# Prologue of a fused attention and MLP kernel: GpSimd normalises the third chunk by add and multiply, two constants are made sooner, and the sums of two tiles stand ahead of their squares

## The chip, the core and the metric

The kernel runs on one core of a Trainium2 chip. A core has five engines that run at the same time, each with its own instruction queue: PE (TensorE, matrix products), DVE (VectorE), ACT (ScalarE), POOL (GpSimd) and SP (SyncE, which here only issues DMAs). An engine takes its instructions strictly in the order in which they stand in its queue; an instruction that waits for another engine holds up everything behind it. The metric is the device time of one execution in microseconds (us), lower is better. Before the change it is 777.7 us, the median of three runs that went from 776.79 to 778.06 us.

## What is computed

The input `x` has 2048 tokens of 512 numbers. The reference is, cut to what matters:

```python
xn = layernorm(x)                                  # over the 512 numbers of a token
q, k, v = heads(xn @ wqkv)                         # 32 heads of 16 numbers
scores = q @ k.T / 4, only for 0 <= i - j < 256    # causal, sliding window of 256 tokens
s = softmax(scores) @ v  (heads joined)  @ wo
g = silu(gelu(layernorm(xn) @ w1 + b1) @ w2 + b2)  # 512 -> 1792 -> 512
out = x + s * g
```

Here only the first line, the projections of the first heads and the first row maxima of their scores matter.

## The kernel before

**Stages.** The tokens are worked on in 4 chunks of 512, a chunk in 4 tiles of 128 tokens (the partitions). The stages are a prologue (some 77 us: layernorm of all chunks, their transposes, the first projections), the attention of eight groups of four heads (to about 420 us), then the MLP and the output. The order on every engine but SP is fixed by hand: instructions stand on their engine in the order in which the program issues them. The prologue runs in time steps `t` = -16 to -1, four for each chunk; `fills` holds the PE work of each step, `plan`, `lns` and `ends` other work at given steps. In step `t` the row maxima of block `m = t + 12` are also made (`max_block`, line 469).

**Numbers in two parts.** Products are made of a high and a low part of each operand. So an array that PE has put into PSUM is copied by ACT (the high part) and then DVE subtracts that from the original (the low part). For a chunk of `xn` these are the ACT `CAST xnT` and the DVE `TENSOR_TENSOR xnT` of the profile.

**Layernorm** (`layernorm`, line 81) gives a tile's steps in one of three ways:

- By DVE's statistics (`each`, line 107): DVE finds mean and variance (`mv`), POOL takes the power -1/2 (`rs`); then `end` (line 139) has ACT, DVE or POOL apply them. For tiles in `on_pool` POOL does it: `(x - mean) * rs`, subtract and multiply, in the profile `x<-x,mvA,rsA`. These are tiles 1 to 3 of the third chunk.
- By sums (`by_sums`): `total` (line 89) has ACT sum the tile and POOL make the negative mean `nm` of it; `squares` (line 94) has ACT sum the squares of `x + nm` and POOL make `rs` of that (`ve`, then a power); `end_sums` (line 101) has POOL make `(x + nm) * rs`, add and multiply, in the profile `x<-x,nmA,rsA`. Tiles 0 and 1 of the second chunk, tile 0 of the third and all four of the last are made so.

The steps of the last chunk (`ln3`) run at `lns` (line 772): tiles 0 and 1 at the end of step -13, tiles 2 and 3 at the end of step -11, each tile's three steps in a row.

**The prologue's buffers.** Chunks 3 and 4 lie in one SBUF tile, `x23`. The transposes of a chunk (`job_x`, line 232) go into PSUM tiles `tr` of a pool of two buffers (`ps_st`, line 190), into `fb`, and for one chunk `zo`; the first halves of V (`job_v`, line 335, PE `pv`, then an ACT copy into `vt`) take turns on the same two `ps_st` buffers. So a `pv` waits until the two parts of the transposes before it are taken out of PSUM, and a transpose waits until the `pv` before it is copied.

**Row maxima** (`max_block`). PE puts scores of a block of 128 queries into `xy` (older keys into `zo`), DVE replaces those above the diagonal (`copy_predicated`, line 488, with the triangle `upper` as the mask) and takes the maximum (`mt<-xy`). Each block overwrites `xy`, so PE waits for the maximum of the block before.

**The two constants.** `upper` begins as all ones: PE multiplies it with itself in 16 products at the start, whose result nobody reads, and ACT copies it into the first q/k slot. Line 690 then makes the triangle of it on POOL. Line 689 puts ones into the last column of `vt`, whose first reader is `clear_part` (line 211) at step -4.

Of the kernel before, what the change touches and what calls it, by code (L numbers as in the profile page):

```python
# [13 lines left out]
ALU = mybir.AluOpType  # L14
# [3 lines left out]
S, D, H, DH, WIN, F = 2048, 512, 32, 16, 256, 1792  # L18
P = 128
# [30 lines left out]
def mixer_kernel(ctx, tc, x, wqk, wv, wo, w1, b1, w2, b2, out):  # L50


    nc = SimpleNamespace(**{name: Ordered(tc, name) for name in ("tensor", "vector", "scalar", "gpsimd", "sync")})
# [27 lines left out]
    def layernorm(ts, name, on_act, eager=False, n_act=4, by_sums=(), on_pool=()):  # L81

        n = len(ts)
        nm = small.tile([P, n], F32, tag="nm", name=f"nm{name}") if by_sums else None
        sums = small.tile([P, n, 2], F32, tag="sums", name=f"sums{name}") if by_sums else None

        def total(i):

            nc.scalar.activation(x23[:, 8], ts[i], AF.Identity, accum_out=sums[:, i, 0:1])
            nc.gpsimd.tensor_scalar(nm[:, i: i + 1], sums[:, i, 0:1], -1.0 / D, None, op0=ALU.mult)

        def squares(i):

            nc.scalar.activation(x23[:, 8], ts[i], AF.Square, bias=nm[:, i: i + 1], accum_out=sums[:, i, 1:2])
            ve = small.tile([P, 1], F32, tag="ve1", name=f"ve{name}_{i}")
            nc.gpsimd.tensor_scalar(ve, sums[:, i, 1:2], 1.0 / D, EPS, op0=ALU.mult, op1=ALU.add)
            nc.gpsimd.tensor_tensor(rs[:, i: i + 1], ve, mhalf[:, :1], op=ALU.pow)

        def end_sums(i):
            nc.gpsimd.tensor_scalar(ts[i], ts[i], nm[:, i: i + 1], rs[:, i: i + 1], op0=ALU.add, op1=ALU.mult)
        mv = small.tile([P, n, 2], F32, tag="mv", name=f"mv{name}")
        rs = small.tile([P, n], F32, tag="rs", name=f"rs{name}")
        sh = small.tile([P, n], F32, tag="shift", name=f"shift{name}")

        def each(i):

            stats(i)
            ve = small.tile([P, 1], F32, tag="ve1", name=f"ve{name}_{i}")  # L110
            nc.vector.tensor_scalar(ve, mv[:, i, 1:2], EPS, None, op0=ALU.add)
            nc.gpsimd.tensor_tensor(rs[:, i: i + 1], ve, mhalf[:, :1], op=ALU.pow)

        def shift(i):
            nc.vector.scalar_tensor_tensor(sh[:, i: i + 1], mv[:, i, 0:1], -1.0, rs[:, i: i + 1],
                                           op0=ALU.mult, op1=ALU.mult)

        def stats(i):
            st = small.tile([P, 6], F32, tag="bn", name=f"bn{name}_{i}")
            nc.vector.bn_stats(st, ts[i])  # L120
            nc.vector.bn_aggr(mv[:, i], st)

        def invert():
            ve = small.tile([P, n], F32, tag="ve", name=f"ve{name}")
            nc.vector.tensor_scalar(ve, mv[:, :, 1], EPS, None, op0=ALU.add)
            nc.gpsimd.tensor_tensor(rs, ve, mhalf[:, :n], op=ALU.pow)

        def shift_all():
            if on_act:
                nc.vector.scalar_tensor_tensor(sh, mv[:, :, 0], -1.0, rs, op0=ALU.mult, op1=ALU.mult)  # L130

        def apply(i, on_act=on_act):
            if on_act:
                nc.scalar.activation(ts[i], ts[i], AF.Identity, bias=sh[:, i: i + 1], scale=rs[:, i: i + 1])
            else:
                nc.vector.tensor_scalar(ts[i], ts[i], mv[:, i, 0:1], rs[:, i: i + 1],
                                        op0=ALU.subtract, op1=ALU.mult)

        def end(i):

            if i in on_pool:
                nc.gpsimd.tensor_scalar(ts[i], ts[i], mv[:, i, 0:1], rs[:, i: i + 1], op0=ALU.subtract, op1=ALU.mult)
                return
            if i < n_act:
                shift(i)
            apply(i, i < n_act)
        if eager:
            return [(lambda i=i: total(i), lambda i=i: squares(i), lambda i=i: end_sums(i)) if i in by_sums else
                    (lambda i=i: each(i), lambda i=i: end(i)) for i in range(n)]
        return [lambda i=i: stats(i) for i in range(n)] + [invert, shift_all] + [lambda i=i: apply(i) for i in range(n)]  # L150
# [48 lines left out]
    vt = vp.tile([P, NKB, 16, DH + 1], F32, name="vt")  # L199
# [16 lines left out]
    upper = const.tile([P, P], F32, name="upper")  # L216
# [39 lines left out]
    def halves(dst_hi, dst_lo, src, part):  # L256

        if part != 1:
            nc.scalar.copy(dst_hi, src)
        if part != 0:  # L260
            nc.vector.tensor_sub(dst_lo, src, dst_hi.bitcast(F32))

    def split_wqk(part=None):
        n, raw = raws["qk"]
        if part != 1:
            wqs[n] = bigp.tile([P, 2, KT, P], F32R, tag=f"wb{n % 2}", name=f"wqb{n}")
        halves(wqs[n][:, 0], wqs[n][:, 1], raw, part)
# [379 lines left out]
    def transpose0(i):  # L647
        for kt in range(KT):
            nc.tensor.transpose(tr0[kt][:, P * i: P * (i + 1)], xs[0][i][:, P * kt: P * (kt + 1)], ident)
        for _ in range(3 if i < 3 else 0):  # L650
            nc.tensor.matmul(zo[:, 0, 0:P], ident, ident, start=True, stop=True)
# [6 lines left out]
            transpose0(i - 1)  # L658
    ln[3][1]()
    transpose0(3)  # L660
    split_wqk(0)
    ln1 = layernorm(xs[1], "A1", True, True, 3, by_sums=(0, 1))
    ln2 = layernorm(xs[2], "A2", True, True, by_sums=(0,), on_pool=(1, 2, 3))
    ln3 = layernorm(xs[3], "A3", True, True, by_sums=range(4))
# [21 lines left out]
        ln2[i][0]()  # L686
    for i in range(4):
        ln2[i][-1]()
    nc.gpsimd.memset(vt[:, :, :, DH: DH + 1], 1.0)
    nc.gpsimd.affine_select(out=upper, in_=upper, pattern=[[1, P]], compare_op=ALU.is_gt,  # L690
                            fill=0.0, base=0, channel_multiplier=-1)
    for i in range(8):
        behind(-14 + i // 4, nc.sync.dma_start, xn_d[i], xs[i // 4][i % 4])

# [74 lines left out]
    fills[16 * NQ, 0] = [(first_h, (0,))]  # L769
    at(16 * NQ, activate_first)  # L770

    lns = {-13: [*ln3[0], *ln3[1]], -11: [*ln3[2], *ln3[3]]}

    def fill_in(t, half):
        now[:] = t, half
# [56 lines left out]
    for f in range(6, NF, 2):  # L832
        t = gp.tile([P, 2, 512], F32, tag="ohl", name=f"hr_{f}", bufs=4)
# [421 lines left out]
```

## Time and profile before

| | before |
|---|---|
| median of three runs | 777.7 us (776.79 to 778.06) |
| span of the profiled execution, first to last instruction | 775.7 us |
| PE busy | 750.1 us, 97% |
| DVE, ACT, POOL busy | 526.2, 437.5, 295.2 us |
| mean granted PE clock | 0.991 |

The profile shows one execution; its span is 2.0 us below the median of the runs, which also hold what lies around the first and the last instruction. A row of the timeline gives start, length, engine, operation, result and operands with shapes, and in brackets how long the engine was idle before and whom it waited for; consecutive rows of one engine may overlap by some hundredths. All rows have the line number of a helper (L42), so they are told apart by their tiles. The table by windows gives each engine's busy time within a stretch, then PE's granted clock as a share of full speed and the DMA engines' busy share.

### The profile page before, as it was taken

Reading aid. Unit: us, or ns where it says so; the run is one execution under the profiler, and the core shown is the slowest. Engines: PE = TensorE matmul, PEld = TensorE weight load, DVE = VectorE, ACT = ScalarE, POOL = GpSimd, SP = SyncE. Lnnn points to the kernel's source line nnn. Section 1 sums busy time; section 2 is a strip of 40 time slices with the busy share of each in tenths; the row PEclk is TensorE's granted clock in tenths of the full one; section 3 lists DMA queues with packets and bytes.
Section 4 is the critical chain, followed back from the end, with each engine's and each line's share of the span. In section 5 each row is a group of like instructions: output and inputs, shape, how many; then the busy total and the mean of one; then the engine's idle time right before and its main releaser. Section 6 shows DMA issues by size and latency. Waiting matters only on the chain.

```text
span 775.7 us, 18801 instructions
## 1 busy us (share of the span) xinstructions
PE 750.1 (97%) x7428; PEld 586.2 (76%) x7428; DVE 526.2 (68%) x834; ACT 437.5 (56%) x742; POOL 295.2 (38%) x591
## 2 busy tenths in 40 slices
PE   9789999999999999999999999999999999999997
PEld 8678666676668887666666677888887888888886
DVE  6567677786876777988876446754647676576473
ACT  6535776777766676678776865444546454342001
POOL 7710666657656465665875810030100200000101
PEclk9879999999999999999999999999999999999999
DMA  7622444765446883455644274541202322243531
GB/s 258 188 54 49 102 97 114 163 149 117 110 92 167 263 259 99 109 130 140 168 142 155 70 250 147 183 167 41 82 9 82 128 68 96 82 150 123 175 95 54
DMA packets 56951, 99.40 MB, mean 128 GB/s; under 512 B 11104, under 2 KB 11360, under 8 KB 56864
## 3 DMA queue, kind: packets, MB, share of 16 engines
q1 hardware_dynamic: 56864, 98.21, 44.0%
q8 instruction: 58, 0.95, 0.5%
q14 instruction: 29, 0.24, 0.1%
HBM read 51.39 MB, written 29.62 MB: 104 GB/s over the span
## 4 chain that ended last, share of the span: by engine, by line
PE 85%; ACT 4%; POOL 4%; DVE 4%; issue 2%; DMA 1%; DVEq 0%; ACTq 0%; POOLq 0%
PE acc L42 19%; PE fb L42 18%; PE zo L42 12%; PE p L42 9%; PE stb L42 8%; PE h L42 6%; PE s L42 6%; PE xy L42 5%; ACT pt L42 3%; PE pv L42 2%; POOL x L42 1%; POOL pt L42 1%; DVE xy L42 1%; POOL rsA L42 1%; DVE mt L42 1%
## 5 line engine op out<-in xcount | busy, mean ns | idle before, releaser
L42 POOL TENSOR_SCALAR_AFFINE_SELECT pt<-pt 128x256 f32<-128x256 f32 x480 | 193.8, 429 | 168.8 <-ACT pt L42 164.9
L42 ACT ACTIVATE pt<-stb 128x768 f32<-128x768 f32 (+1 forms) x244 | 188.7, 773 | 55.2 <-PE stb L42 45.9
L42 DVE TENSOR_REDUCE mt<-xy 128x4 f32<-128x1024 f32 (+1 forms) x128 | 152.6, 1192 | 4.4
L42 PE MATMUL acc<-w,gh 128*128 128x512 f32 x432 | 134.6, 393 | 0.0
L42 DVE COPY_PREDICATED xy<-upper,zo 128x512 f32<-128x512 int32 x112 | 77.5, 692 | 70.5 <-PE zo L42 69.9
L42 PE MATMUL fb<-xnT,wqb 64*128 64x512 f32 (+1 forms) x684 | 115.2, 404 | 0.8 <-DVE xnT L42 0.8
L42 PE MATMUL zo<-pt,vt 128*17 128x128 f32 x2880 | 103.9, 275 | 1.6 <-DVE xy L42 1.2
L42 PE MATMUL stb<-qk 64*128 64x384 f32 (+1 forms) x488 | 96.8, 393 | 7.4 <-ACT pt L42 5.8
L42 POOL TENSOR_TENSOR xo<-xo,gated 128x512 f32<-128x512 f32 x15 | 20.3, 1350 | 218.9 <-DVE gated L42 215.3
L42 PEld LDWEIGHTS zo<-pt,vt 128*17 128x17 f32 x2880 | 67.4, 97 | 38.7 <-issue 17.7
L42 PEld LDWEIGHTS acc<-w,gh 128*128 128x128 f32 x432 | 80.9, 188 | 17.2
L42 PEld LDWEIGHTS stb<-qk 64*128 64x128 f32 x488 | 45.5, 183 | 53.1 <-ACT pt L42 42.1
L42 PE MATMUL acc<-w,gl 128*128 128x512 f32 x216 | 84.4, 391 | 0.1
L42 PEld LDWEIGHTS fb<-xnT,wqb 64*128 64x128 f32 (+1 forms) x684 | 63.4, 186 | 7.8 <-DVE xnT L42 1.2
L42 PE MATMUL xy<-qk 64*128 64x256 f32 (+2 forms) x536 | 62.0, 306 | 3.6 <-DVE mt L42 3.4
L42 ACT COPY oraw<-zo 128x128 f32<-128x128 f32 x128 | 34.1, 267 | 40.0 <-PE zo L42 35.6
L42 PEld LDWEIGHTS xy<-qk 64*128 64x128 f32 x536 | 44.3, 187 | 14.9 <-DVE mt L42 8.2
L42 PEld LDWEIGHTS acc<-w,gl 128*128 128x128 f32 x216 | 40.5, 188 | 9.6 <-DVE gl L42 0.6
L42 ACT ACTIVATE gated<-acc 128x512 f32<-128x512 f32 x16 | 8.7, 596 | 64.7 <-DVE acc L42 64.7
L42 PE MATMUL s<-wos,ohl 128*128 128x512 f32 (+1 forms) x204 | 44.8, 378 | 0.0
L42 PEld LDWEIGHTS s<-wos,ohl 128*128 128x128 f32 x204 | 36.7, 188 | 7.1
L42 PE MATMUL zo<-qk 64*128 64x128 f32 x448 | 40.6, 259 | 0.0
(190 smaller groups left out, 1173.1 us busy)
## 6 DMA issues: line engine op xcount, KB each, us to landing
qk<-sh SPq DMA_DIRECT2D x128, 128.0 KB
qk<-pjr SPq DMA_DIRECT2D x64, 128.0 KB
oT_d<-oraw SPq DMA_DIRECT2D x32, 256.0 KB
w_d<-in_w_dram SPq DMA_DIRECT2D x14, 512.0 KB
x<-in_x_dram SPq DMA_DIRECT2D x16, 256.0 KB
or<-oT_d SPq DMA_DIRECT2D x16, 256.0 KB
w<-rden_d SPq DMA_DIRECT2D x16, 256.0 KB
xo<-in_x_dram SPq DMA_DIRECT2D x16, 256.0 KB
```

The lines of the kernel that those rows point to most:

```text
L42: r = issue(*args, **kwargs)
```

## The change

Three edits, none of which alters what is computed:

1. Tiles 1 to 3 of the third chunk: POOL first makes `nm` = -1 * mean (a 128x1 operation), then uses `end_sums`, so add and multiply take the place of subtract and multiply.
2. The ones in `vt` and the triangle `upper` are issued right after the first chunk's transposes, ahead of all other layernorms, and no longer behind the third chunk's.
3. In the last chunk, two tiles go together: both sums, then the first tile's squares and end, then the second's.

```diff
         def end(i):
             if i in on_pool:
-                nc.gpsimd.tensor_scalar(ts[i], ts[i], mv[:, i, 0:1], rs[:, i: i + 1], op0=ALU.subtract, op1=ALU.mult)
+                nc.gpsimd.tensor_scalar(nm[:, i: i + 1], mv[:, i, 0:1], -1.0, None, op0=ALU.mult)
+                end_sums(i)
                 return
...
     ln[3][1]()
     transpose0(3)
+    nc.gpsimd.memset(vt[:, :, :, DH: DH + 1], 1.0)
+    nc.gpsimd.affine_select(out=upper, in_=upper, pattern=[[1, P]], compare_op=ALU.is_gt,
+                            fill=0.0, base=0, channel_multiplier=-1)
     split_wqk(0)
...
     for i in range(4):
         ln2[i][-1]()
-    nc.gpsimd.memset(vt[:, :, :, DH: DH + 1], 1.0)
-    nc.gpsimd.affine_select(out=upper, in_=upper, pattern=[[1, P]], compare_op=ALU.is_gt,
-                            fill=0.0, base=0, channel_multiplier=-1)
...
-    lns = {-13: [*ln3[0], *ln3[1]], -11: [*ln3[2], *ln3[3]]}
+    lns = {t: [ln3[i][0], ln3[i + 1][0], *ln3[i][1:], *ln3[i + 1][1:]] for t, i in ((-13, 0), (-11, 2))}
```

The queues of PE, DVE and SP keep their order; those of POOL and ACT change. On POOL, from the end of the third chunk to the first two tiles of the last one; `x_90` is a tile of `x23`, the numbers behind other names only tell tiles apart. Before:

```order
35 L42 TENSOR_SCALAR x_90<-x_90,nmA_236,rsA_239 128x512
36 L42 TENSOR_SCALAR x_90<-x_90,mvA_238,rsA_239 128x512 x3
37 L42 MEMSET vt 128x256
38 L42 AFFINE_SELECT upper<-upper 128x128
39 L42 TENSOR_SCALAR nmA_241<-sumsA_242 128x1
40 L42 TENSOR_SCALAR veA_0_426<-sumsA_242 128x1
41 L42 TENSOR_TENSOR rsA_244<-veA_0_426,mhalf 128x1
42 L42 TENSOR_SCALAR x_90<-x_90,nmA_241,rsA_244 128x512
43 L42 TENSOR_SCALAR nmA_241<-sumsA_242 128x1
```

After, the same place on POOL:

```order
37 L42 TENSOR_SCALAR x_90<-x_90,nmA_238,rsA_241 128x512
38 L42 TENSOR_SCALAR nmA_238<-mvA_240 128x1
39 L42 TENSOR_SCALAR x_90<-x_90,nmA_238,rsA_241 128x512
40 L42 TENSOR_SCALAR nmA_238<-mvA_240 128x1
41 L42 TENSOR_SCALAR x_90<-x_90,nmA_238,rsA_241 128x512
42 L42 TENSOR_SCALAR nmA_238<-mvA_240 128x1
43 L42 TENSOR_SCALAR x_90<-x_90,nmA_238,rsA_241 128x512
44 L42 TENSOR_SCALAR nmA_243<-sumsA_244 128x1 x2
45 L42 TENSOR_SCALAR veA_0_431<-sumsA_244 128x1
46 L42 TENSOR_TENSOR rsA_246<-veA_0_431,mhalf 128x1
47 L42 TENSOR_SCALAR x_90<-x_90,nmA_243,rsA_246 128x512
48 L42 TENSOR_SCALAR veA_1_436<-sumsA_244 128x1
```

The three normalisations have become pairs of a small and a large operation, the two constants are gone from here, and the last chunk's first two `nm` stand together, ahead of the first tile's `ve`.

The constants now stand earlier on POOL, between the last power of the first chunk and the first `nm` of the second chunk. After:

```order
15 L42 TENSOR_TENSOR rsA_171<-veA_3_212,mhalf 128x1
16 L42 MEMSET vt 128x256
17 L42 AFFINE_SELECT upper<-upper 128x128
18 L42 TENSOR_SCALAR nmA_233<-sumsA_234 128x1
19 L42 TENSOR_TENSOR wqb_231<-wqkr_146,wqb_231 128x512
20 L42 TENSOR_TENSOR wva<-wvr_0_148,wva 128x512
```

Before, the same rows without rows 16 and 17 stood there. On ACT, the last chunk's sums (results `x_90,sumsA`, operand `x_90` alone) and squares (operand `nmA` as well), with the copies that stand between the two pairs; before:

```order
25 L42 ACTIVATE x_90,sumsA_242<-x_90 128x512
26 L42 ACTIVATE x_90,sumsA_242<-x_90,nmA_241 128x512
27 L42 ACTIVATE x_90,sumsA_242<-x_90 128x512
28 L42 ACTIVATE x_90,sumsA_242<-x_90,nmA_241 128x512
29 L42 CAST sh_1_453<-fb_107 128x512
30 L42 COPY vt<-pv_2_468 128x32x16
31 L42 ACTIVATE x_90,sumsA_242<-x_90 128x512
32 L42 ACTIVATE x_90,sumsA_242<-x_90,nmA_241 128x512
33 L42 ACTIVATE x_90,sumsA_242<-x_90 128x512
34 L42 ACTIVATE x_90,sumsA_242<-x_90,nmA_241 128x512
35 L42 CAST xnT<-tr_0_516 128x512
```

After, the same place on ACT:

```order
25 L42 ACTIVATE x_90,sumsA_244<-x_90 128x512 x2
26 L42 ACTIVATE x_90,sumsA_244<-x_90,nmA_243 128x512 x2
27 L42 CAST sh_1_456<-fb_107 128x512
28 L42 COPY vt<-pv_2_471 128x32x16
29 L42 ACTIVATE x_90,sumsA_244<-x_90 128x512 x2
30 L42 ACTIVATE x_90,sumsA_244<-x_90,nmA_243 128x512 x2
31 L42 CAST xnT<-tr_0_519 128x512
```

Within each pair, the second tile's sum has moved ahead of the first tile's squares; the copies between the pairs stand where they stood.

## The prediction

> **What bounds the kernel now.** First the page's line of busy times, then the table by windows, to see where PE is not busy:
>
> ```profile
> PE 750.1 (97%) x7428; PEld 586.2 (76%) x7428; DVE 526.2 (68%) x834; ACT 437.5 (56%) x742; POOL 295.2 (38%) x591
> ```
>
> ```profile
> 31.00:36.00 5.00, 1.36 (x10) 0.99 (x11) 2.05 (x4) 3.63 (x9) 2.75 (x8) 0.82 0.36 136
> 36.00:42.00 6.00, 3.94 (x21) 3.42 (x21) 2.89 (x4) 4.24 (x12) 3.76 (x9) 0.50 0.61 134
> ...
> 47.00:52.00 5.00, 4.54 (x28) 3.50 (x28) 3.58 (x7) 0.59 (x1) 0.00 (x0) 0.92 0.00 0
> ...
> 78.00:200.00 122.00, 118.55 (x1711) 83.00 (x1709) 92.33 (x126) 88.65 (x151) 78.38 (x169) 1.00 0.52 123
> ```
>
> PE sets the time: 97% over the span, 118.55 of 122 us from 78 to 200. But from 31 to 42 it works 5.3 of 11 us, and the column behind POOL shows its clock at 0.50 of full speed. From the means, it was at half speed for 5 x 0.18 / 0.5 = 1.8 us of the first window and 0.8 us of the one from 47 to 52, so from about 34.2 to 47.8. Hence what is gained before 48 us counts in full, if PE then goes on as before. The timeline shows who makes PE wait:
>
> ```profile
> 23.90 6.24 POOL L42 TENSOR_SCALAR x<-x,mvA,rsA 128x512 f32<-128x512 f32 x3
> 27.08 3.13 PE L42 MATMUL pv<-wva,xnT 128*128 128x256 f32 x24
> 27.77 2.49 SPq L42 DMA_DIRECT2D xn_d<-x  x4
> 30.08 0.55 POOL L42 MEMSET vt<- 128x256 f32 x1
> 30.76 0.25 POOL L42 TENSOR_SCALAR nmA<-sumsA 128x1 f32<-128x1 f32 x1
> 30.82 0.75 DVE L42 COPY_PREDICATED_SCALAR xy<-upper,negc 128x512 f32 x1 [5.32 <-POOL upper L42]
> 31.05 0.72 ACT L42 ACTIVATE x<-x,nmA 128x512 f32<-128x512 f32 x1 [6.36 <-POOL nmA L42]
> 31.89 0.63 ACT L42 ACTIVATE x<-x 128x512 f32<-128x512 f32 x1
> 31.95 0.19 POOL L42 TENSOR_SCALAR veA<-sumsA 128x1 f32<-128x1 f32 x1 [0.93 <-ACT x L42]
> 32.22 0.57 POOL L42 TENSOR_TENSOR rsA<-veA,mhalf 128x1 f32<-128x1 f32 x1
> 32.36 0.50 PE L42 MATMUL xy<-qk 64*128 64x256 f32 x4 [2.15 <-DVE mt L42]
> 32.79 0.65 PE L42 MATMUL tr<-ident,x 128*128 128x128 f32 x4
> 32.90 0.77 POOL L42 TENSOR_SCALAR x<-x,nmA,rsA 128x512 f32<-128x512 f32 x1
> 35.09 0.59 ACT L42 COPY vt<-pv 128x512 f32<-128x512 f32 x1
> 35.57 0.64 ACT L42 ACTIVATE x<-x 128x512 f32<-128x512 f32 x1
> 35.73 1.11 PE L42 MATMUL tr<-ident,x 128*128 128x128 f32 x4 [2.28 <-ACT vt L42]
> 36.63 1.91 PE L42 MATMUL fb<-ident,x 128*128 128x128 f32 x8
> 39.59 0.72 ACT L42 ACTIVATE x<-x,nmA 128x512 f32<-128x512 f32 x1 [1.27 <-POOL nmA L42]
> 40.31 1.05 ACT L42 CAST xnT<-tr 128x512 fp32r<-128x512 f32 x2
> 40.91 1.29 DVE L42 TENSOR_TENSOR xnT<-tr,xnT 128x512 fp32r<-128x512 f32 x2 [3.08 <-ACT xnT L42]
> 41.66 5.49 PE L42 MATMUL pv<-wva,xnT 128*128 128x256 f32 x24 [2.06 <-DVE xnT L42]
> 43.31 0.69 DVE L42 COPY_PREDICATED xy<-upper,zo 128x512 f32<-128x512 int32 x1
> ```
>
> PE waits three times. At 30.2 for the first block's maximum, which waits for the triangle `upper`, queued on POOL behind the third chunk. At 33.4 for the V copy on ACT, queued behind squares that wait for POOL's `nm`. At 39.6 for the two parts of the last-made transposes, on ACT behind the last squares. All three lead back to POOL, busy without a break until 31.0. The 24 `pv` products then take 5.49 us at half clock, against 3.13 at full.
>
> **Edit 1, add for subtract.** POOL's groups, shapes kept apart:
>
> ```profile
> L42 POOL TENSOR_SCALAR x<-x,mvA,rsA 128x512 f32<-128x512 f32 x3 | 6.2, 2094 | 0.0
> L42 POOL TENSOR_SCALAR x<-x,nmA,rsA 128x512 f32<-128x512 f32 x7 | 5.4, 773 | 0.4
> L42 POOL TENSOR_SCALAR nmA<-sumsA 128x1 f32<-128x1 f32 x7 | 1.8, 258 | 1.8 <-ACT x L42 1.8
> ```
>
> The changed operation is the second row's to the letter (add, multiply, both operands made on POOL), so I take 0.77 us for 2.09. Each tile also gets a small operation, 0.26 by the third row, with some 0.08 before the large one can use it (`ve` ends at 32.14, its reader starts at 32.22). A tile then costs about 1.1 us, three 3.25, against 6.24: 3.0 us of POOL. Bounds: 0.19 for the small one (the `ve` row) gives 3.2; 2.09 for the large one unchanged gives a loss of 1.0 (a rival below).
>
> **Edit 2, the constants.** Behind the third chunk they took from 30.08 to 30.76, 0.7 us, now gone there. So the third chunk ends, and the last chunk's first `nm` starts, at 23.90 + 3.25 = 27.15 instead of 30.76. In their new place:
>
> ```profile
> 7.80 0.55 POOL L42 TENSOR_TENSOR rsA<-veA,mhalf 128x1 f32<-128x1 f32 x1 [0.52 <-DVE shiftA L42]
> 8.39 0.55 DVE L42 TENSOR_SCALAR x<-x,mvA,rsA 128x512 f32<-128x512 f32 x1 [0.60 <-POOL rsA L42]
> 8.85 0.75 DVE L42 CAST wva<-wvr 128x512 fp32r<-128x512 f32 x2
> 10.14 0.23 POOL L42 TENSOR_SCALAR nmA<-sumsA 128x1 f32<-128x1 f32 x1 [1.79 <-ACT x L42]
> 18.41 1.01 DVE L42 TENSOR_SCALAR x<-x,mvA,rsA 128x512 f32<-128x512 f32 x1 [0.67 <-POOL rsA L42]
> 19.11 0.40 POOL L42 TENSOR_SCALAR nmA<-sumsA 128x1 f32<-128x1 f32 x1
> ```
>
> POOL is free from 8.35 and idle 1.79 us until ACT's sum is ready at 10.1. The 0.7 us fit, on paper at no cost, and hide in that gap. Without that cover they would delay the whole POOL queue, which from 10.14 to 30.8 has few breaks. One thing speaks for a little: DVE's normalisation took 0.55 us alone, 1.01 beside a POOL operation of that size, and POOL's small operation behind it 0.40 in place of 0.26. DVE works from 8.39 to 9.60. If POOL gives way all that time, the constants end at 9.60 + 0.7 = 10.3, 0.2 late. Bounds 0 to 0.4; I take 0, since below 0.24 it costs nothing later (next part).
> The Trainium skill (SBUF — State Buffer, "SBUF: two separate sides") says that VectorE and GpSimd share a port pair as an exclusive lock, in which the later one blocks fully. By that rule the sum would lose up to the 0.2 us just worked out; the rows at 18.41 and 19.11 agree with it.
> With the triangle ready near 9, DVE masks the first block when its scores are there (about 27.1) and PE's wait at 30.2 goes.
>
> **Edit 3, sums ahead of squares,** and the sum from there:
>
> ```profile
> 48.14 0.70 DVE L42 COPY_PREDICATED xy<-upper,zo 128x512 f32<-128x512 int32 x1 [2.29 <-PE zo L42]
> 48.87 1.23 DVE L42 TENSOR_REDUCE mt<-xy 128x4 f32<-128x1024 f32 x1
> 50.15 0.50 PE L42 MATMUL xy<-qk 64*128 64x256 f32 x4 [0.47 <-DVE mt L42]
> 50.87 0.70 DVE L42 COPY_PREDICATED xy<-upper,zo 128x512 f32<-128x512 int32 x1
> ```
>
> A sum or squares takes ACT about 0.84 us at most (31.05 to 31.89). Before, ACT waited 1.3 us for POOL at each tile; now the second sum and its `nm` are done meanwhile.
> 1. First squares at 27.15 + 0.29 (30.76 to 31.05) = 27.44, second at 28.28, ACT free at 29.1. The wait added for the second sum, which stands ahead of the first squares, is none: ACT was idle 6.36 us there.
> 2. The V copy is now bound by its own products, which end at 30.21: it runs from 30.25. Behind it two sums, 30.73 (35.57 follows 35.09 by 0.48) to 32.2 (0.72 each, as from 39.59 to 40.31).
> 3. POOL: `ve` 0.90 after the squares, 28.34; power, normalisation at 29.3 (0.95 after `ve`, 31.95 to 32.90); second tile's at 31.0 to 31.75; third `nm` done by 31.95. So ACT's next squares start at 32.2, bound by ACT, with 0.24 to spare for a late POOL.
> 4. Squares 32.2 and 33.03; cast of the transposes 0.72 later (39.59 to 40.31), 33.75; DVE 0.60 later, 34.35; PE's `pv` 0.75 later, **35.1** instead of 41.66.
> 5. Meanwhile PE: scores of block 1 at 30.2, transposes behind them, at full clock until about 32.9 (0.43, 0.65, 0.65 and half of 1.91). Block 1's maximum takes until 32.8 (mask and maximum 2.01, 48.14 to 50.15). Block 2's scores follow, to 33.6. PE then idles 1.5 us.
> 6. If the clock holds, `pv` ends at 35.1 + 3.13 = 38.2. Block 2's maximum: DVE masks it 2.40 after 34.35 (40.91 to 43.31), maximum at 38.76, where PE takes block 3; DVE masks that 0.72 later (50.15 to 50.87), 39.48; block 4 at 39.48 + 2.01 = **41.5** instead of 50.15.
>
> The gain is 50.15 - 41.5 = 8.7 us: 6.56 until `pv`, 2.1 more from its clock. SP keeps its order; its transfers of chunk 2's q/k rows now follow the stores of `xn` at 30.3 (27.77 + 2.49), no longer ACT's cast near 35. The table has the DMA engines 36% busy from 31 to 36, and block 4 needs the rows at 41.5. After 50 us all rows depend on each other alone, so they move together. So the profiled execution's span goes from 775.7 to 767.0, and the median, 2.0 us above, from 777.7 to **769.0**.
>
> **Rivals.**
> *The clock falls again.* Before, it fell at 34.2 after PE had worked 1.1 of some 4 us since 30.2, of which 0.65 transposes. Now from 30.2 to 35.1 PE works 3.4 of 4.9 us, but only about 1.1 us of these are scores, the rest transposes. If it falls, `pv` takes 5.49 and block 4 comes as long after it as before: the gain is 41.66 - 35.1 = 6.56, 771.1 us. For it: the scores' share is hardly more than before. Against: PE's longest rest is 1.5 us, not 2.3, and all its work fills two thirds of the time.
> By the Trainium skill (TensorE: Matmul & The Clock Gate, "Part 4: PE-mode transpose") transposes do not count as busy in the way that products do, which leads to 771.1. The same page's first part says that the clock falls after an idle window of about 3.4 us, by which it would stay; here it fell without one idle stretch that long, so that rule differs from this trace.
> *The clock falls and stays down.* Each us at half clock costs 0.5 us of PE's work. The gain is used up when it comes back (35.1 + 2 x 8.66) = 52.4 or later; back at 60, the time is 777.7 + 3.8 = 781.5. Against it: before, it came back 6.1 us after `pv` began.
> *The 2.09 us belongs to the place, not to the subtraction* (that tile, busy DMAs). Then the third chunk ends at 27.15 + 3 x 1.32 = 31.1; by steps 1 to 4, now with POOL's waits, `pv` starts at 38.9, at half clock: a gain of 2.8, 774.9 us. Against it: the seven rows of 0.77, one of which is this chunk's first tile.
> *A later stage takes it back,* waiting for a transfer as late as before: 777.7. No PE wait after 78 us speaks for it.
>
> **Chances.** Clock holds 0.50; falls 0.37; stays down 0.03; place 0.05; taken back 0.05. The likeliest is 769.0. The range takes in the second case with 0.8 us for the spread of the runs (0.7) and the 0.2 of the port: up to 771.9; down to 767.7, for waits that shrink more than I count. What a measurement can tell is 0.2%, 1.6 us: faster 0.50 + 0.37 + 0.05 = 0.92, same 0.05, slower 0.03.
>
> **What would show it.** Right: three `x<-x,nmA` rows of 0.77 behind 23.9; no PE wait for the first maximum; `pv` at 35 and of 3.1 us; block 4 at 41.5; no clock of 0.50 between 34 and 48. A `pv` of 5.5 us shows the first rival, rows of 2.1 the third, a late `nm` at 10.1 the port. `pv` after 37, or a new wait between 42 and 78 us, would make the prediction wrong.

## The result, and the profile after

The changed kernel takes 769.83 us, the median of four runs (769.18 to 770.34), against 777.27 us before, here the median of four runs (776.79 to 778.06): a ratio of 0.9903, interval 0.9889 to 0.9917, or 7.4 us less. The forecast was 769.0 us (767.7 to 771.9), a gain of 8.7 us. The profiled execution has a span of 767.5 us, 8.2 less than before. The page's first line, and the table by windows:

```profile
PE 745.8 (97%) x7428; PEld 582.5 (76%) x7428; DVE 526.5 (69%) x834; ACT 437.3 (57%) x742; POOL 291.1 (38%) x594
```

```profile
31.00:36.00 5.00, 2.94 (x28) 2.56 (x28) 3.14 (x5) 4.78 (x13) 3.40 (x9) 1.00 0.97 313
36.00:42.00 6.00, 5.01 (x39) 4.13 (x38) 5.72 (x9) 1.29 (x3) 0.82 (x2) 1.00 0.05 11
...
47.00:52.00 5.00, 4.76 (x43) 4.29 (x42) 4.03 (x5) 2.74 (x5) 0.00 (x0) 1.00 0.54 118
...
78.00:200.00 122.00, 118.28 (x1776) 83.77 (x1770) 93.30 (x128) 87.90 (x152) 78.77 (x171) 1.00 0.54 127
```

PE now works 8.0 of the 11 us from 31 to 42, where it worked 5.3, and its clock is 1.00 in every window shown. From 78 us on PE is as busy as before, 118.28 of 122 us. The timeline of the stage that changed:

```profile
24.11 0.23 POOL L42 TENSOR_SCALAR nmA<-mvA 128x1 f32<-128x1 f32 x1
24.44 0.77 POOL L42 TENSOR_SCALAR x<-x,nmA,rsA 128x512 f32<-128x512 f32 x1
25.49 0.77 POOL L42 TENSOR_SCALAR x<-x,nmA,rsA 128x512 f32<-128x512 f32 x1
26.53 0.77 POOL L42 TENSOR_SCALAR x<-x,nmA,rsA 128x512 f32<-128x512 f32 x1
27.27 0.37 POOL L42 TENSOR_SCALAR nmA<-sumsA 128x1 f32<-128x1 f32 x2
27.31 3.13 PE L42 MATMUL pv<-wva,xnT 128*128 128x256 f32 x24
27.43 0.75 DVE L42 COPY_PREDICATED_SCALAR xy<-upper,negc 128x512 f32 x1 [1.69 <-PE xy L42]
27.51 0.72 ACT L42 ACTIVATE x<-x,nmA 128x512 f32<-128x512 f32 x1 [1.82 <-POOL nmA L42]
30.37 0.50 PE L42 MATMUL xy<-qk 64*128 64x256 f32 x4
30.48 0.59 ACT L42 COPY vt<-pv 128x512 f32<-128x512 f32 x1 [0.78 <-PE pv L42]
30.96 0.63 ACT L42 ACTIVATE x<-x 128x512 f32<-128x512 f32 x1
31.72 0.63 ACT L42 ACTIVATE x<-x 128x512 f32<-128x512 f32 x1
32.53 0.72 ACT L42 ACTIVATE x<-x,nmA 128x512 f32<-128x512 f32 x1
33.44 0.72 ACT L42 ACTIVATE x<-x,nmA 128x512 f32<-128x512 f32 x1
34.16 1.05 ACT L42 CAST xnT<-tr 128x512 fp32r<-128x512 f32 x2
35.50 3.13 PE L42 MATMUL pv<-wva,xnT 128*128 128x256 f32 x24 [1.84 <-DVE xnT L42]
39.16 0.50 PE L42 MATMUL xy<-qk 64*128 64x256 f32 x4 [0.52 <-DVE mt L42]
41.89 0.51 PE L42 MATMUL xy<-qk 64*128 64x256 f32 x4 [0.47 <-DVE mt L42]
```

Three things are to be seen. POOL's three normalisations take 0.77 us each, and the last chunk's first `nm` comes at 27.27 instead of 30.76. Of PE's three waits only one is left, 1.84 us ahead of `pv`; ACT's four sums and squares ahead of the cast now run with at most 0.2 us between them, so ACT and no longer POOL makes it. And `pv` takes 3.13 us, not 5.49. Block 4 begins at 41.89, 8.3 us sooner; the spans differ by 8.2. The earlier `pv`, which no edit touches, began at 27.31 instead of 27.08: this execution was 0.23 late already before the changed stage. (POOL's first `nm` of the second chunk, which waits for ACT's sum, came at 10.40 instead of 10.14.)

The constants in their new place, on POOL, with DVE beside them:

```profile
8.58 0.55 POOL L42 MEMSET vt<- 128x256 f32 x1
8.66 0.74 DVE L42 TENSOR_SCALAR x<-x,mvA,rsA 128x512 f32<-128x512 f32 x1 [0.60 <-POOL rsA L42]
8.98 0.56 POOL L42 TENSOR_SCALAR_AFFINE_SELECT upper<-upper 128x128 f32<-128x128 f32 x1
9.32 0.83 DVE L42 CAST wva<-wvr 128x512 fp32r<-128x512 f32 x2
10.40 0.23 POOL L42 TENSOR_SCALAR nmA<-sumsA 128x1 f32<-128x1 f32 x1 [0.85 <-ACT x L42]
```

Before, the triangle stood alone, with no DVE work beside it:

```profile
30.49 0.30 POOL L42 TENSOR_SCALAR_AFFINE_SELECT upper<-upper 128x128 f32<-128x128 f32 x1
```

Now they meet: DVE's two groups take 0.74 and 0.83 in place of 0.55 and 0.75, the triangle 0.56 in place of 0.30. But POOL is then still idle 0.85 us until ACT's sum, so the meeting costs nothing. In all seven traces with the constants in this place, those of the experiments included, POOL is idle there for 0.58 to 1.43 us.

### The profile page after: what moved, and what is told of

Same layout as the page of the kernel before. It is cut to its first block, busy times and chain, and to the rows that moved or that the text cites. A ratio compares the mean times of both kernels' runs of the same rounds, so it can differ in the third digit from the quotient of the medians.

```text
span 767.5 us, 18809 instructions
## 1 busy us (share of the span) xinstructions
PE 745.8 (97%) x7428; PEld 582.5 (76%) x7428; DVE 526.5 (69%) x834; ACT 437.3 (57%) x742; POOL 291.1 (38%) x594
## 4 chain that ended last, share of the span: by engine, by line
PE 86%; ACT 5%; DVE 4%; POOL 3%; issue 2%; ACTq 0%; DVEq 0%; POOLq 0%
PE acc L42 19%; PE fb L42 18%; PE zo L42 13%; PE p L42 9%; PE stb L42 8%; PE h L42 6%; PE s L42 6%; PE xy L42 5%; ACT pt L42 3%; PE pv L42 2%; POOL pt L42 1%; DVE xy L42 1%; DVE mt L42 1%; PE yt L42 1%; POOL rsA L42 1%
## 5 line engine op out<-in xcount | busy, mean ns | idle before, releaser
L42 ACT COPY p<-p 128x512 f32<-128x512 f32 x21 | 12.3, 585 | 50.1 <-PE p L42 42.8
```

What stands on the lines that cost most here:

```text
L42: r = issue(*args, **kwargs)
```

## The experiments

**The theory** is the one on record: POOL, then ACT, DVE and PE form a chain; the edits shorten POOL's part and ACT's waits for POOL, and a busier PE keeps its clock. **The rivals:** the clock does most of it; each PE wait counts for itself; POOL alone binds, whatever the order; the slow part of `subtract` is its operand.

The first table puts together the profiles by one measure that is free of a late start: the time from the untouched `pv` to the next one (27.08 to 41.66 before). A gain in time is worked out from the ratio to runs of the kernel before, measured beside each kernel, with its interval; it can differ by up to half a us from the difference of the medians.

| kernel | pv to pv, us | less than before | median, us | gain, us |
|---|---|---|---|---|
| before | 14.58 | | | |
| edit 1 alone | 11.42 | 3.2 | 773.93 | 2.8 (1.8 to 3.8) |
| edit 2 alone | 13.86 | 0.7 | 776.81 | 0.5 (-0.2 to 1.3) |
| edit 3 alone | 11.54 | 3.0 | 773.35 | 3.6 (2.4 to 4.7) |
| 2 and 3, without 1 | 10.89 | 3.7 | 773.72 | 3.8 (2.6 to 4.9) |
| 1 and 3, without 2 | 8.44 | 6.1 | 770.60 | 7.0 (5.8 to 8.3) |
| 1 and 2, without 3 | 10.76 | 3.8 | 773.02 | 4.4 (3.2 to 5.5) |
| all three | 8.19 | 6.4 | 769.83 | 7.5 (6.5 to 8.6) |

In the profiles of all six kernels with one or two edits the clock fell, for 3.4 to 6.8 us in all.

**Edit 1 alone.**

```diff
-  (in_ - mean) * rs                       # gpsimd: subtract, mult
+  nm = -1 * mean;  (in_ + nm) * rs        # gpsimd: mult; add, mult
```

> Only edit 1 (the negative mean made on POOL, then add and multiply); constants and order of sums as before. The theory on record (a chain POOL -> ACT -> DVE -> PE, bound by POOL): the third chunk ends 3.0 us sooner, the constants and the last chunk's first nm with it; each of ACT's waits for POOL stays, so the pv products start near 38.7 instead of 41.66, after a PE rest of over 3 us, hence at half clock: 2.9 us faster than before. Rival (the clock does most of it, and any shorter wait keeps it): over 4.5 us faster, pv of 3.1 us.

773.93 us against 776.88, ratio 0.9964 (0.9951 to 0.9977). PE's rows:

```profile
28.08 3.13 PE L42 MATMUL pv<-wva,xnT 128*128 128x256 f32 x24
...
33.59 0.65 PE L42 MATMUL tr<-ident,x 128*128 128x128 f32 x4 [1.36 <-ACT vt L42]
...
39.50 4.63 PE L42 MATMUL pv<-wva,xnT 128*128 128x256 f32 x24 [3.08 <-DVE xnT L42]
```

The waits for ACT stay, one of them, through DVE, now 3.08 us, and `pv` runs partly at half clock (4.63). The gain is the theory's; over 4.5 us is out.

**Edit 2 alone.**

```diff
     transpose0(3)
+    (ones of vt, triangle of upper)
...
-    (ones of vt, triangle of upper)       # behind the third chunk
```

> Only edit 2 (ones and triangle made early). The theory on record: PE's wait for the first maximum (2.15 us) goes, but the next wait, for the V copy on ACT, grows by nearly as much, since POOL reaches the last chunk only 0.65 us sooner: pv near 41.0, 0.6 us faster than before, which can't be told from none. Rival (each PE wait counts for itself): 2.1 us faster.

776.81 us against 776.88, ratio 0.9993 (0.9983 to 1.0003): no difference that can be told, and 2.1 us is out.

```profile
30.96 0.66 PE L42 MATMUL tr<-ident,x 128*128 128x128 f32 x4
35.41 1.12 PE L42 MATMUL tr<-ident,x 128*128 128x128 f32 x4 [3.79 <-ACT vt L42]
```

PE's 2.15 us wait for the first maximum is gone, and the next one has grown from 2.28 to 3.79: a wait removed ahead of a later one on the same chain is only moved.

**Edit 3 alone.**

```diff
-    -13: [*ln3[0], *ln3[1]]
+    -13: [ln3[0][0], ln3[1][0], *ln3[0][1:], *ln3[1][1:]]      # -11 likewise
```

> Only edit 3 (the sums of two tiles ahead of their squares). The theory on record: the first nm at 30.8 as before, but ACT's wait for POOL between two tiles goes in both pairs (1.3 us each, and what POOL needs less): pv near 38.5 at half clock, 3.1 us faster than before. Rival (ACT's waits are hidden behind POOL, which still has the same work): under 1 us faster.

773.35 us against 776.88, ratio 0.9954 (0.9939 to 0.9969). The wait for the triangle stays (2.13 us in its trace), and still `pv` comes 3.0 us sooner after the one before it. That POOL's work alone binds is out: the order counts as much as the 3 us of edit 1.

**Two of three.** Each leaves out one of the edits above.

> Edits 2 and 3 without edit 1 (subtract and multiply, 2.1 us a tile). The theory on record: the last chunk's first nm at 30.1, pv near 37.9 at half clock: 3.7 us faster than before, half of the whole change. Rival (the third chunk's time is hidden, the order of the sums does it all): as fast as the changed kernel, 7.4 us faster than before.

773.72 us against 777.41, ratio 0.9951 (0.9937 to 0.9966): as expected, the third chunk's time is not hidden.

> Edits 1 and 3, the constants where they were, behind the third chunk. The theory on record: the 0.7 us of the constants delay POOL's chain, of which 0.24 us is slack on ACT: pv near 36.0, 0.5 us slower than the changed kernel; the first maximum is still ready by 30.2. Rival (PE's wait for the triangle counts on its own): over 1.5 us slower than the changed kernel.

770.60 us against 777.41, ratio 0.9910 (0.9893 to 0.9926). By the trace, `pv` comes 0.25 us later than with all three (8.44 against 8.19); in time this can't be told from the changed kernel. So by the traces edit 2 is worth 0.25 us there, half of what was expected, and 0.7 alone.

> Edits 1 and 2, each tile's sum and squares in a row as before. The theory on record: ACT waits 1.3 us for POOL at each tile, pv near 38.0, 3.6 us faster than before if the clock falls, 5.3 if it holds. Rival (POOL alone binds, and it has the same work in another order): as fast as the changed kernel.

773.02 us against 777.41, ratio 0.9944 (0.9929 to 0.9959): ACT's waits for POOL are worth 2.6 us of the way to `pv` (10.76 against 8.19). In this profile the clock fell (`pv` 5.49 us).

**Subtraction or operand.** The changed kernel with

```diff
-  nm = -1 * mean;  (in_ + nm) * rs
+  nm = 1 * mean;   (in_ - nm) * rs        # both on gpsimd, operand made on gpsimd
```

> The changed kernel, but POOL's small operation copies the mean (times 1) and the large one subtracts and multiplies, with both operands made on POOL. If subtraction itself is the slow part: three rows of 2.1 us, the first nm near 31.2, some 2.8 us faster than before. If an operand made by DVE, or its stride, was the slow part: rows of 0.77 us and the time of the changed kernel, 7.4 us faster than before.

774.64 us against 777.41, ratio 0.9962 (0.9947 to 0.9977): 3.0 us faster, where 2.8 were expected if subtraction is the slow part. POOL's rows:

```profile
23.55 0.77 POOL L42 TENSOR_SCALAR x<-x,nmA,rsA 128x512 f32<-128x512 f32 x1
24.28 0.23 POOL L42 TENSOR_SCALAR nmA<-mvA 128x1 f32<-128x1 f32 x1
24.61 2.11 POOL L42 TENSOR_SCALAR x<-x,nmA,rsA 128x512 f32<-128x512 f32 x1
```

The first is add and multiply, the third subtract and multiply: same SBUF tile, both operands made on POOL, 0.77 and 2.11 us. It is the subtraction.

**What transposes count for, and what the clock is worth.** The kernel before, with idle work on PE in its three rests; the second kernel has 16 transposes wherever this one has 8 products:

```diff
+    def busy_pe(n):
+        for _ in range(n):
+            nc.tensor.matmul(zo[:, 0, 256:384], ident, ident, start=True, stop=True)
...
+    busy_pe(8)        # ahead of block 1's scores; of the transposes' second quarter; of pv
```

> The kernel before, with 8 idle products of 128x128 (into a part of PSUM that nobody reads) in each of PE's three rests from 30 to 42 us; every wait stays. If the clock falls for want of work on PE, it now stays at 1.00; pv starts at 41.7 as before but takes 3.1 us: 2.1 us faster than before. Rival (the clock falls for another reason, or pv of 3.1 us is given back at the next maximum): no faster.

> The kernel before, with 16 idle transposes of 128x128 in each of PE's three rests from 30 to 42 us, of about the same length as the 8 products of the other kernel. If all work on PE counts for the clock, it holds as with the products: 2.1 us faster than before. If transposes don't count, the clock falls near 34 as before, pv takes 5.5 us, and the time is that of before.

781.78 and 781.44 us against 777.38, ratios 1.0055 (1.0040 to 1.0070) and 1.0054 (1.0037 to 1.0071), both slower, and neither expectation met. The row of the last filler, with products, shows why:

```profile
44.24 3.78 PE L42 MATMUL zo<-ident 128*128 128x128 f32 x16 [5.47 <-DVE xy L42]
```

It writes the tile `zo`, which DVE's mask was still to read, and so waited 5.47 us: a flaw of the experiment. Up to there, the two still tell the question apart. PE and its clock with transposes:

```profile
30.19 1.91 PE L42 MATMUL zo<-ident 128*128 128x128 f32 x16
32.45 0.50 PE L42 MATMUL xy<-qk 64*128 64x256 f32 x4 [0.35 <-DVE mt L42]
32.89 0.65 PE L42 MATMUL tr<-ident,x 128*128 128x128 f32 x4
33.38 1.91 PE L42 MATMUL zo<-ident 128*128 128x128 f32 x16
35.82 0.66 PE L42 MATMUL tr<-ident,x 128*128 128x128 f32 x4 [0.53 <-ACT vt L42]
```

```profile
34.00:35.00 1.00, 1.00 (x11) 1.00 0.00 0
...
43.00:44.00 1.00, 0.00 (x0) 0.52 0.02 8
...
49.00:50.00 1.00, 1.00 (x7) 0.57 0.00 0
```

From 30.2 to 38.0 only 0.5 us of PE's work are products, the rest transposes, and the clock stays at 1.00 through 34, where it fell before; it falls at 43.0, as in the kernel with products, after both had rested over 4 us. So transposes count. The trace of the experiment above, with subtraction, shows the same the other way round. There the clock was at half from 33.88 to 37.29, and PE did nothing but transposes in that time, up to 37.23; then the clock came back:

```profile
34.48 1.11 PE L42 MATMUL tr<-ident,x 128*128 128x128 f32 x4 [2.58 <-ACT vt L42]
35.39 1.91 PE L42 MATMUL fb<-ident,x 128*128 128x128 f32 x8
```

The repaired form, with no filler behind a mask:

```diff
-    busy_pe(8)        # ahead of pv
+    busy_pe(10)       # between block 2's newer and older scores
```

> The kernel before with idle products of 128x128 on PE, into a part of PSUM that nobody reads: 8 ahead of block 1's scores, 8 ahead of the second quarter of the third chunk's transposes, 10 between block 2's newer and older scores. Unlike the first attempt, none stands behind a mask of DVE. Every wait of the kernel before stays. If want of work on PE lets the clock fall, it now stays at 1.00 in every run, pv starts at 41.7 as before and takes 3.1 us, block 3's maximum then binds: 2.1 us faster than a run of before with 13.6 us at half clock, some 1.5 us faster than its median. Rival (the clock is worth nothing, since pv is covered by the next maximum): no faster.

775.97 us against 777.10, ratio 0.9985 (0.9976 to 0.9994).

```profile
41.98 3.13 PE L42 MATMUL pv<-wva,xnT 128*128 128x256 f32 x24 [0.45 <-DVE xnT L42]
...
48.37 0.50 PE L42 MATMUL xy<-qk 64*128 64x256 f32 x4 [0.47 <-DVE mt L42]
```

The way from `pv` to `pv` stays at 14.54 us (14.58 before), and the clock alone is worth 1.2 us (0.5 to 1.9); some 1.5 were expected. From `pv` to block 4 it takes 6.39 us, against 8.49 in the profile of before. The 11 runs had mean clocks of 0.998 to 1.000 and lie within 0.7 us.

**The changed kernel again,** word for word.

> The changed kernel once more, word for word, for more executions. If the clock falls in some of them after PE's rest of 1.84 us, some runs have a mean clock of 0.995 to 0.997 and are 0.5 to 1.5 us slower than those with 0.999 or 1.000; the median is 7.4 us faster than before. If the clock has no part in the spread, time and clock are unrelated.

769.77 us against 777.10, ratio 0.9904 (0.9890 to 0.9917). This time the profile caught the clock falling:

```profile
35.87 4.31 PE L42 MATMUL pv<-wva,xnT 128*128 128x256 f32 x24 [1.85 <-DVE xnT L42]
...
43.13 0.50 PE L42 MATMUL xy<-qk 64*128 64x256 f32 x4 [0.49 <-DVE mt L42]
```

```profile
37.00:38.00 1.00, 1.00 (x8) 0.68 0.09 25
38.00:39.00 1.00, 1.00 (x7) 0.50 0.00 0
...
40.00:41.00 1.00, 1.00 (x9) 0.61 0.00 0
```

It was down from 37.4 to 40.8, and `pv` took 1.2 us more, of which 0.5 were to be waited for the maximum anyway. Of all eight runs of the changed kernel, the four with a mean clock of 0.999 or 1.000 took 769.2 to 769.9, the four with 0.996 to 0.998 took 769.6 to 770.6. The two groups overlap, so that the price of a fall, some 0.5 us by their means, is only roughly known.

**A faster version.** The one rest left is ACT's: take its last two tiles out of the way of the cast.

```diff
-    lns = {... for t, i in ((-13, 0), (-11, 2))}
+    lns = {... for t, i in ((-13, 0), (-10, 2))}
```

> The changed kernel, with the sums, squares and normalisations of the last chunk's tiles 2 and 3 one step later (-10 in place of -11), so that on ACT the four casts of the third chunk's transposes stand ahead of them. If PE's last rest of 1.84 us before pv is due to ACT's two sums and two squares ahead of the cast, pv starts near 33.7 instead of 35.5, bound by PE and DVE, and the kernel is 1.8 us faster than the changed one (about 9.3 us faster than before). Rival (the weight cast behind these squares on ACT becomes late and holds DVE's next mask): under 0.8 us faster than the changed one.

768.06 us against 776.88, ratio 0.9887 (0.9872 to 0.9902), 8.8 us faster than before (7.6 to 9.9). That is 1.3 us more than the changed kernel's 7.5, and the two medians differ by 1.8 us; but the two kernels were not measured side by side, and the intervals overlap. The traces show the step itself:

```profile
28.05 3.13 PE L42 MATMUL pv<-wva,xnT 128*128 128x256 f32 x24
...
34.32 3.13 PE L42 MATMUL pv<-wva,xnT 128*128 128x256 f32 x24
37.97 0.50 PE L42 MATMUL xy<-qk 64*128 64x256 f32 x4 [0.52 <-DVE mt L42]
...
40.83 0.51 PE L42 MATMUL xy<-qk 64*128 64x256 f32 x4 [0.61 <-DVE mt L42]
```

`pv` now waits for nothing, 6.27 us after the one before, and block 4 comes 12.78 us after that one, against 14.58 in the changed kernel: 1.8 us, as expected. The clock was 0.999 or 1.000 in all four runs. What is left to wait for up to block 4 is DVE's maxima, at most 0.6 us each; the late weight cast of the rival costs some 0.1 of that (2.86 us from block 3 to block 4, against 2.73).

## Why the prediction was right, point by point

- *The bound.* Right: what PE gained before 48 us came through to the end, 8.3 us at block 4 and 8.2 in the span. Nothing was taken back later.
- *Edit 1.* Right: 1.05 us a tile (24.44, 25.49, 26.53), 1.1 forecast; the subtraction, not the place, was slow.
- *Edit 2.* Right in its main value, no cost in the new place, and in its reason, POOL's idle time. The meeting with DVE stretched the triangle by 0.26 us, with 0.85 to spare. The lock on a shared port pair that the Trainium skill states (SBUF — State Buffer, "SBUF: two separate sides") fits the stretched rows on both engines; the 0.2 us by that rule were not lost. With the other two edits in place, 0.25 us of the 0.7 that this edit takes out of POOL's queue reached `pv`; by steps 1 to 3, with POOL 0.24 to spare, it would have been 0.46.
- *Edit 3, steps 1 to 4.* Right but 0.2 short: `pv` was forecast for 35.1 and came at 35.50, of which 0.23 is the late start. ACT's sums and squares took 0.76, 0.81 and 0.91 us from start to start in place of 0.72, 0.72 and 0.83. As forecast, ACT and not POOL bound here.
- *Step 6, the clock.* Here the size was off. 2.1 us were counted for it, from one execution of before with a mean clock of 0.991; over the runs the clock alone is worth 1.2 us (0.5 to 1.9). Of 43 executions of before beside the experiments, those with 0.990 have a mean of 777.8 us, those with 0.993 of 776.9, so the profile had caught one of the slower ones. With 6.4 for the way to `pv` and 1.2 for the clock the sum is 7.6, and 7.4 to 7.5 was measured. The time came closer to the forecast than the gain did, 0.8 us off against 1.3, and that is luck: before took 777.27 us here, 0.4 less than the 777.7 that the forecast was counted from.
- *The first rival.* It was put as one or the other; in fact the clock held in four of eight runs and fell in four. That the profile of the result shows it held at 1.00, as forecast, is therefore partly luck. A fall lasts 3.4 us in the trace that shows it, and costs 0.9 us by that trace (7.26 from `pv` to block 4, against 6.39) and some 0.5 by the runs, not 2.1. Its reason, that transposes might not count, is out. The Trainium skill's sentence to that effect (TensorE: Matmul & The Clock Gate, "Part 4: PE-mode transpose") does not hold in this case: 16 transposes in each gap kept the clock as 8 products did.
- *The other rivals.* None came: no clock that stays down, no slow place, no gain given back. The q/k transfers began at 30.57, where 30.3 was forecast.

## What to carry to other kernels

When PE waits several times along one chain of engines, cost the whole chain to the last wait: here taking away the wait that was easiest to see (2.15 us) gained 0.5 us by itself, which can't be told from nothing, and the order of the sums on ACT gained 3.6. Look for operations of one shape with two durations, as POOL's 2.09 and 0.77 here, since the form of an expression may be free. And take a clock's price from several executions: a profile shows only one.

## What the hardware showed beyond that

- On POOL, subtract and multiply of 128x512 takes 2.1 us, whether DVE or POOL made the mean (2.09 and 2.11). Add and multiply takes 0.77, here always with operands made on POOL.
- The spells at half clock had one length or multiples of it in all eleven traces that have any: 3.41 us in seven (as in the changed kernel, 37.4 to 40.8), 6.83 in three (as with transposes in the gaps, 43.0 to 49.8), 13.65 before (34.2 to 47.8). With edit 2 alone there were two of 3.41, and 3.41 between them. The Trainium skill (TensorE: Matmul & The Clock Gate, "Part 1: The HAM clock gate (the "warmup" mystery)") gives a window of 3.4 us that runs freely; these lengths agree with it.
- The clock can fall when PE is already at work again: in the changed kernel it did so 1.5 us after `pv` had begun. What the falls have in common is how busy PE was in the 3.41 us ahead of them: 46% at most in all twelve (32% before, 46% in the changed kernel). If windows of this length are laid out from the falls, from 22 to 58 us of the same traces, the clock held after every window at full clock in which PE was 51% busy or more, and once after one of 45%. It came back after windows at half clock that were 82% busy or more, and stayed down after those of 81% or less.
- So a short rest can be enough. The last one of the changed kernel, 1.84 us, leaves 46% of a window that holds all of it, and more of two that share it. This would explain why the clock falls in some executions and not in others; it is argued, not shown, since a trace without a fall doesn't show where its windows lie.
